# Two layers of hedgehog attention and mish: phi_q turned into tiles of its own, and five blocks of the first layer turned by VectorE

## The chip, the core and the metric

The kernel runs on one core of one Trainium2 chip. A core has TensorE (PE), which multiplies and writes to PSUM; VectorE (DVE), ScalarE (ACT) and GpSimd (POOL), which work elementwise; and SyncE (SP), whose queue issues all of this kernel's transfers. Every engine executes its own instructions in order and waits on semaphores for the others. The metric is device time of one execution in microseconds; of several runs the median counts.

## What is computed

Two identical layers follow each other on x (2048 tokens, 640 columns, fp32). Each is an attention step A and a dense step B, both with a residual and a layer norm ahead:

```python
x = x + _A_ref(_layernorm(x), A_wqkv, A_w_phi, A_wo)
x = x + _B_ref(_layernorm(x), B_w1, B_b1, B_w2)

def _A_ref(x, wqkv, w_phi, wo):              # 32 heads of 20 columns
    q, k, v = heads of x @ wqkv
    pq, pk = q @ w_phi, k @ w_phi            # per head
    phi_q = concat([softmax(pq), softmax(-pq)])
    phi_k = concat([softmax(pk), softmax(-pk)])
    kv, z = phi_k^T v, sum over tokens of phi_k
    return heads joined of (phi_q kv) / (phi_q z) @ wo

def _B_ref(x, w1, b1, w2):                   # 1536 hidden columns
    h = x @ w1 + b1
    return (h * tanh(softplus(h))) @ w2
```

## The kernel before

The 2048 tokens are worked in NB = 8 blocks of BLK = 256, and each block in BT = 2 tiles of 128 tokens (numbered i = 0 to 15). Weights and inputs are split into a high and a low part, and each product is made of three matmuls, so a projection of one token tile is 30 matmuls over 320 columns (`project`, L329; `project_half`, L338, whose matmul is L344).

A projection needs the normalized rows with the 640 columns on the partitions, that is, transposed. There are two ways to that:

- `normed` (L299) normalizes a block's rows on ACT into two row tiles `xn`, and `Transposed.step` (L271) transposes them on TensorE, 128 x 128 at a time (L280), ten transposes per block, into a PSUM tile `one`. ACT copies it to the high part `xth`, and VectorE subtracts to the low part `xtl` (L286).
- `spill_turned` (L311) transposes rows on VectorE within blocks of 32 x 32 (L315) and puts the blocks in their places by eight stores to DRAM in runs of 128 bytes (L317); `load_turned` (L319) reads them back in three loads (L325), and `Transposed.step` then takes `xth` and `xtl` from these SBUF tiles.

In the first layer's attention all eight blocks go the first way. In the second layer they go the second way: the end of the dense step before writes them (`n2_d`).

Each attention has two halves. `attend_first` (L381) goes over the blocks; in each, six steps project keys, values and queries of both token tiles (k0, k1, v0, v1, q0, q1; blocks 0 and 1 in other orders). What follows a projection is cut into stages by generators that are held in `pending`, and `advance` (L393) takes each one stage further after every step. `features` (L355) is shared by keys and queries: ACT copies the projection out of PSUM, VectorE takes maximum and minimum of every head (L368), two subtractions follow (L369 and L371), ACT exponentiates, VectorE sums (L377) and inverts (L378), and GpSimd multiplies (L379). For a key tile, 11 matmuls then add to the sums over tokens (L416). For a query tile, VectorE transposes the 128 x 1280 tile in place in 32 x 32 blocks (L425), and four stores of 160 KB each in runs of 128 bytes (L429) bring it to its block's tensor `e_d` in DRAM. Two query tiles (`r2_wide`, names `r210` and `r211`) take turns.

`attend_second` (L553) first finishes the sums (`finish_kv`, L532) and then, block by block, reads a block of `e_d` into two tiles of 1280 columns and a small one (`load`, L521), multiplies it with the sums and divides (`average`, L562, matmul L573), transposes the result on TensorE and projects it with wo. Loads of several blocks are under way ahead. The last queries (`rest`) are spread over its first steps.

What sets the order: ACT's work on the chain runs in program order (`act`, L110, chains each activation to the one before). All of the program stands in one block that the scheduler orders for each engine from its own model of the times. Inside `attend_second`, and in the opening of the first layer for SP, a hand-written order holds instead for TensorE and SP.

Buffers that take turns: `big` (1280 columns) has five, used for key tiles and for the loaded halves of `e_d`; `ol` (512 columns) has six; `x` (rows of a block) two; `xn` (640 columns) four; `mm`, the PSUM tile of a projection, two, and `one` four.

Of the kernel before, what the change touches and what calls it, by code (L numbers as in the profile page):

```python
# [42 lines left out]
def kernel(  # L43
# [266 lines left out]

    def spill_turned(rows, dst):  # L311

        dst = dst.rearrange("(j f) (t q s) -> t q f j s", f=32, t=BT, s=32)
        for t in range(BT):
            nc.vector.transpose(rows[t], rows[t])  # L315
            for q in range(4):
                nc.sync.dma_start(dst[t, q], rows[t][32 * q:32 * q + 32].rearrange("f (j s) -> f j s", s=32))  # L317

# [68 lines left out]
    def attend_first(layer, x_src, first):  # L387


        def fetch_normed(b):  # L390
            if layer:
                return load_turned(n2_d[b], [row_tile] * 3)
            xt = fetch(x_src, b)  # L393
            norm_scale(b, [norm_stats(t, xt) for t in range(BT)])
            return xt

        pending = []

        def advance():
# [21 lines left out]
        def queries(xts, i, ps=None):  # L421
            e = query_tile(i)
            yield from features(project(xts, i % BT, q_ws, 0) if ps is None else ps, e, True)

            nc.vector.transpose(e, e)  # L425
            b, t = divmod(i, BT)
            dst = e_d[b].rearrange("(j f) (t q s) -> t q f j s", f=32, t=BT, s=32)
            for q in range(4):
                nc.sync.dma_start(dst[t, q], e[32 * q:32 * q + 32].rearrange("f (j s) -> f j s", s=32))  # L429
                if b == NB - 1:  # L430
                    yield

        def values(xts, i, v):
# [30 lines left out]
        for b in range(NB):  # L464
# [9 lines left out]
            for n, (kind, t) in enumerate(order):  # L474
# [46 lines left out]
    def load(b):  # L521

        ta, tb, tc_ = big_tile(), big_tile(), pair_tile(F32)
        for t, g0 in ((ta, 0), (tb, 5)):

            src = e_d[b][120 * g0:120 * (g0 + 4) + P]
            src = bass.AP(tensor=src.tensor, offset=src.offset, ap=[[BLK, P], [120 * BLK, 5], [1, BLK]])
            nc.sync.dma_start(t.rearrange("f (g s) -> f g s", s=BLK), src)
        nc.sync.dma_start(tc_[:80, 0], e_d[b][1200:])
        return [(ta, tb)[g // 5][:, (g % 5) * BLK:(g % 5 + 1) * BLK] for g in range(10)] + [tc_[:, 0]]  # L530

    def finish_kv(kva, kvz, mask):  # L532

        acc, acz = row_tile(), row_tile()
        for src, dst, p1, n, w in ((kva, acc, P, 4, 120), (kvz, acz, P, 1, 120), (kvz, acz, 42, 1, 80)):
            c = 120 if w == 80 else 0
            nc.vector.tensor_tensor(dst[:p1, c:c + n * w].rearrange("p (n w) -> p n w", n=n),
                                    src[:p1, c:c + n * w].rearrange("p (n w) -> p n w", n=n),
                                    mask[:p1, :w].unsqueeze(1).to_broadcast([p1, n, w]), op=ALU.mult)
        yield  # L540
        for src, q0, n in ((acc, 0, 4), (acz, 4, 2)):
            ps = one_tile().rearrange("p (n c) -> p n c", n=4)
            for q in range(n):
                p1, w = (P, 120) if q0 + q < 5 else (42, 80)
                nc.tensor.transpose(ps[:w, q, :p1], src[:p1, 120 * q:120 * q + w], ident[:p1, :p1])  # L545
            if n == 4:
                act(kvb[:, :4], ps[:120], AF.Copy)
            else:
                nc.vector.tensor_copy(kvb[:, 4], ps[:120, 0])
                nc.vector.tensor_copy(kvb[:80, 5, :42], ps[:80, 1, :42])  # L550
        yield

    def attend_second(x_src, x_dst, acc, fetches, makes, fetch_next, begin_next):  # L553
# [9 lines left out]
        def average(b, t):  # L563
# [3 lines left out]
            for g in range(G):  # L567
                n = 120 if g < 10 else 80
                w = GW if g < 10 else 42
                c, j = divmod(g, 8)  # L570
                for q in range(2):
                    s0 = t * P + 64 * q
                    nc.tensor.matmul(  # L573
                        po[64 * q:64 * q + 64, c, GW * j:GW * j + w], phs[g][:n, s0:s0 + 64],
                        kvb[:n, g // 2, 64 * (g % 2):64 * (g % 2) + w], start=True, stop=True)
# [105 lines left out]
    def dense(x_src, x_dst, w1s, w2s, first, last):  # L681
# [58 lines left out]
        def end(b):  # L740
# [21 lines left out]
            if not last:  # L762
                xn = [row_tile() for _ in range(BT)]
                normalize(b, xn, [xt[:, t, :] for t in range(BT)])
                spill_turned(xn, n2_d[b])

# [132 lines left out]
```

## Time and profile before

| | us |
|---|---|
| runs, median of 3 | 1398.32 (1397.06 to 1398.65) |
| the profiled execution | 1396.09 |
| its span | 1394.3 |
| first layer: first half of attention | 0 to about 265 |
| first layer: second half of attention | about 265 to 375 |
| first layer: dense step | about 375 to 720 |
| second layer: first half of attention | about 720 to 942 |
| second layer: second half of attention | 942 to 1052 |
| second layer: dense step | 1052 to 1394 |

The profile shows one execution. Its rows give the start or the busy time in us, the engine, the line of the kernel, the operation, what it writes and reads (out<-in, by the names of the program), the shape, and the count; in brackets stands the idle time of the engine ahead of it and what ended it. "mean ns" follows the busy time where rows are grouped. The groups of the page that name the tiles of this change:

```profile
L280 PE MATMUL one<-ident,xn 128*128 128x128 f32 x260 | 37.2, 279 | 0.0
L429 SPq DMA_DIRECT2D e_d<-r x128: 302/885/3631, 59.6 to 1001.7; - x128
L317 SPq DMA_DIRECT2D n_d<-xn x176: 302/537/2272, 385.9 to 1317.1; - x176
```

The first is a group by form, with busy us and mean ns; matmuls are pipelined, so that the mean is longer than the pitch. The other two are the queue's own rows by line: shortest, median and longest time of one issue in ns, and the first and last start.

### The profile page before, as it was taken

The page shows a single profiled execution, that of the slowest core. Times are in us where ns is not written, and L with a number is a line of the kernel's source. Part 1 is how long each engine was busy: PE and PEld are TensorE (multiplying, and loading weights), DVE is VectorE, ACT ScalarE, POOL GpSimd, SP SyncE. Part 2 cuts the span into 40 slices and gives each one's busy share as a digit, 9 for nine tenths or more (in the row PEclk, how much of TensorE's full clock was granted, in tenths as well). Part 3 has the DMA queues.
Part 4 walks back from the last instruction along what each step waited for, and adds up shares of the span by engine and source line. Part 5 has one row for each costly group of instructions (what it writes and reads, how often), then busy time and mean ns, then how long its engine had stood idle before and what let it go on. Part 6 is the DMA issues. An engine that isn't in the chain of part 4 may idle for free. (4 is left out here: it accounts for less than half of the span.)

```text
span 1394.3 us, 28137 instructions
## 1 busy us (share of the span) xinstructions
PE 1380.7 (99%) x11528; PEld 1367.0 (98%) x11528; DVE 1075.5 (77%) x1820; ACT 583.3 (42%) x973; POOL 440.0 (32%) x334
## 2 busy tenths in 40 slices
PE   7999999999999999999999999999999999999998
PEld 7999999999999999999999999999999999999998
DVE  5797877796698877788769988888767876777775
ACT  4444433321355454545454333332235444444443
POOL 1353443343422221222234434343342211211112
PEclk9999999999999999999999999999999999999999
DMA  8533333689633432343474333357976212333200
GB/s 328 162 79 54 67 52 58 184 228 307 235 86 95 114 84 62 83 114 95 122 261 87 71 57 58 65 107 231 288 257 200 76 25 72 95 95 95 75 22 20
DMA packets 350035, 169.57 MB, mean 122 GB/s; under 512 B 286866, under 2 KB 323458, under 8 KB 349906
## 3 DMA queue, kind: packets, MB, share of 16 engines
q1 hardware_dynamic: 349906, 167.78, 44.2%
q8 instruction: 90, 1.47, 0.4%
q14 instruction: 39, 0.32, 0.1%
HBM read 104.82 MB, written 62.91 MB: 120 GB/s over the span
## 5 line engine op out<-in xcount | busy, mean ns | idle before, releaser
L737 PE MATMUL mm<-r2h,ol 128*128 128x320 f32 x1280 | 304.7, 309 | 0.0
L721 POOL TENSOR_TENSOR ol<-big,ol 128x512 fp32r<-128x512 f32 (+1 forms) x98 | 129.8, 1324 | 483.5 <-ACT ol L720 407.3
L695 PE MATMUL one<-xtl,r1h 128*128 128x256 f32 x960 | 268.2, 279 | 0.0
L695 PE MATMUL one<-xth,r1l 128*128 128x256 f32 x960 | 268.0, 279 | 0.0
L695 PE MATMUL one<-xth,r1h 128*128 128x256 f32 x960 | 265.9, 279 | 0.0
L737 PEld LDWEIGHTS mm<-r2h,ol 128*128 128x128 f32 x1280 | 219.1, 188 | 0.0
L737 PE MATMUL mm<-r2l,ol 128*128 128x320 f32 x640 | 197.3, 309 | 0.0
L344 PE MATMUL mm<-r1h,xth 128*128 128x320 f32 x600 | 187.3, 312 | 0.0
L344 PE MATMUL mm<-r1h,xtl 128*128 128x320 f32 x600 | 186.0, 310 | 0.7 <-DVE xtl L286 0.7
L344 PE MATMUL mm<-r1l,xth 128*128 128x320 f32 x600 | 186.0, 310 | 0.0
L695 PEld LDWEIGHTS one<-xtl,r1h 128*128 128x128 f32 x960 | 180.4, 188 | 0.0
L695 PEld LDWEIGHTS one<-xth,r1l 128*128 128x128 f32 x960 | 180.4, 188 | 0.0
L695 PEld LDWEIGHTS one<-xth,r1h 128*128 128x128 f32 x960 | 179.6, 188 | 0.0
L710 DVE TENSOR_SCALAR big<-big 128x512 f32<-128x512 f32 (+1 forms) x98 | 57.1, 583 | 109.9 <-ACT big L708 109.7
L379 POOL TENSOR_TENSOR r<-r,r 128x1280 f32<-128x1280 f32 x32 | 75.8, 2368 | 163.1 <-DVE r L378 157.3
L737 PEld LDWEIGHTS mm<-r2l,ol 128*128 128x128 f32 x640 | 120.2, 188 | 0.0
L712 ACT ACTIVATE big<-big,two 128x512 f32<-128x512 f32 (+1 forms) x98 | 70.1, 715 | 116.2 <-DVE big L711 116.1
L708 ACT ACTIVATE big<-one,b1s 128x256 f32<-128x256 f32 x192 | 80.8, 467 | 90.1 <-PE one L695 89.6
L720 ACT ACTIVATE ol<-big 128x512 fp32r<-128x512 f32 (+1 forms) x98 | 61.0, 622 | 136.0 <-DVE big L719 135.9
L344 PEld LDWEIGHTS mm<-r1h,xth 128*128 128x128 f32 x600 | 112.8, 188 | 1.3
L344 PEld LDWEIGHTS mm<-r1h,xtl 128*128 128x128 f32 x600 | 112.7, 188 | 1.3 <-DVE xtl L286 1.0
L344 PEld LDWEIGHTS mm<-r1l,xth 128*128 128x128 f32 x600 | 112.8, 188 | 0.1
(129 smaller groups left out, 3156.1 us busy)
## 6 DMA issues: line engine op xcount, KB each, us to landing
e_d<-r SPq DMA_DIRECT2D x128, 160.0 KB, 4.0
big<-e_d SPq DMA_DIRECT2D x32, 640.0 KB, 6.6
x_d<-xt SPq DMA_DIRECT2D x23, 640.0 KB, 3.9
xt<-x_d SPq DMA_DIRECT2D x22, 640.0 KB, 4.3
n_d<-xn SPq DMA_DIRECT2D x176, 80.0 KB, 2.1
xt<-in_x SPq DMA_DIRECT2D x16, 640.0 KB, 5.9
xn<-x_d SPq DMA_DIRECT2D x28, 320.0 KB, 4.2
v<-n_d SPq DMA_DIRECT2D x30, 256.0 KB, 3.3
```

What stands on the lines that cost most here:

```text
L344: nc.tensor.matmul(ps[:, :HC], a[:, sl], r, start=(k == 0 and n == 0), stop=(k == KD - 1 and n == 2))
L379: nc.gpsimd.tensor_tensor(eg, eg, r.unsqueeze(2).to_broadcast([P, 2 * H, DH]), op=ALU.mult)
L695: nc.tensor.matmul(ph[:, j, :], l, r, start=(n == 0), stop=(n == 3 * KD - 1))
L708: exps[0] = nc.scalar.activation(part(ta, 0)[:, j - js.start], ph[:, j, :], AF.Exp, bias=b1s[:, 2 * pr + j:2 * pr + j + 1]).ins
L710: nc.vector.tensor_scalar_min(e, e, E_CAP)
L712: nc.scalar.activation(r, n, AF.Ln, bias=two)
L720: nc.scalar.activation(ah[:, js], n, AF.Copy)
L721: nc.gpsimd.tensor_tensor(al[:, js], n, ah[:, js].bitcast(F32), op=ALU.subtract)
L737: nc.tensor.matmul(pys[t][:, c, :HC], l[:, j, sl], r, start=(f == 0 and n == 0), stop=(f == KF - 1 and n == 2))
```

## The change

In both layers:

- Query tiles of blocks 0 to 6 are no longer transposed in place. When the first tile of a block is ready, three tiles are taken (`blocks[b]`: two of the `big` buffers and 192 columns of an `ol` buffer), and VectorE transposes each query tile in three pieces into them, two of 640 columns (four blocks of 32 for each of five groups, the groups 120 columns apart, so that 8 columns are read twice) and one of 96, with strided sources and destinations (L476 of the changed kernel). After the block's second tile, twelve stores bring the three tiles to `e_d` and `f_d` in runs of 1280 and 256 bytes. Block 7 goes as before, to a tensor `g_d`.
- `load` reads blocks 0 to 6 as whole tiles, in runs of 5120 bytes; the last group has 96 rows instead of 80, the 16 others being met by zeros, for which `finish_kv` clears 16 columns.
- The tokens of a block stand in another order on the way, so `spill_turned` has a form for these tensors, and an input block that is transposed on TensorE is fetched in four transfers by 32 partitions.

In the first layer's attention alone:

- Blocks 0 to 2 are normalized and transposed on TensorE as before. Blocks 3 to 7 go through `turn`: rows are fetched, measured, normalized in place, transposed by VectorE and spilled to `n0_d` three blocks ahead of use, in stages that stand in the steps of the blocks between, and are then loaded as in the second layer.

```diff
+    def row_parts(t, b):
+        return t[b * BLK:(b + 1) * BLK, :].rearrange("(h t s u) d -> u h s t d", h=2, t=BT, u=2)
...
-    e_d = [dram.tile([EW, BLK], F32, name=f"e_d{b}") for b in range(NB)]
+    e_d = [dram.tile([2, P, EW], F32, name=f"e_d{b}") for b in range(NB - 1)]
+    f_d = [dram.tile([96, BLK], F32, name=f"f_d{b}") for b in range(NB - 1)]
+    g_d = dram.tile([EW, BLK], F32, name="g_d")
+    n0_d = [dram.tile([D, BLK], F32, name=f"n0_d{b}") for b in range(NB)]
...
     def attend_first(layer, x_src, first):
+        def fetch_parts(b):
+            xt = x_tile()
+            for q in range(4):
+                nc.sync.dma_start(xt[32 * q:32 * q + 32], row_parts(x_src, b)[q // 2, q % 2])
+            return xt
+
+        def turned(b):
+            return layer or b > 2
+
+        def turn(b):
+            xt = fetch(x_src, b)
+            yield
+            norm_scale(b, [norm_stats(t, xt) for t in range(BT)])
+            yield
+            rows = [xt[:, t, :] for t in range(BT)]
+            normalize(b, rows, rows)
+            yield
+            spill_turned(rows, n0_d[b], True)
+            yield
+
         def fetch_normed(b):
-            if layer:
-                return load_turned(n2_d[b], [row_tile] * 3)
-            xt = fetch(x_src, b)
+            if turned(b):
+                return load_turned((n2_d if layer else n0_d)[b], [row_tile] * 3)
+            xt = fetch_parts(b)
...
         def queries(xts, i, ps=None):
...
+            if t == 0:
+                blocks[b] = [big_tile(), big_tile(), pair_tile(F32).rearrange("p j s -> p (j s)")[:, :192]]
+            for c, dst in enumerate(blocks[b]):
+                src = e[:, EW - 96:].rearrange("p (j f) -> p j f", f=32)
+                if c < 2:
+                    src = e[:, 600 * c:600 * c + 600]
+                    src = bass.AP(tensor=src.tensor, offset=src.offset, ap=[src.ap[0], [32, 4], [120, 5], [1, 32]])
+                    dst = dst.rearrange("p (m g t s) -> p t m g s", m=4, t=BT, s=32)[:, t]
+                else:
+                    dst = dst.rearrange("p (j t s) -> p t j s", t=BT, s=32)[:, t]
+                nc.vector.transpose(dst, src)
+            if t == BT - 1:
+                for q in range(4):
+                    qs = slice(32 * q, 32 * q + 32)
+                    for c, (src, dst, m) in enumerate(zip(blocks[b], (e_d[b][0], e_d[b][1], f_d[b]), (4, 4, 3))):
+                        nc.sync.dma_start(dst.rearrange("(m f) (q x) -> q f m x", m=m, q=4)[q],
+                                          src[qs].rearrange("f (m x) -> f m x", m=m))
+                del blocks[b]
...
                     if n == 0:
                         xt = fetch_normed(b + 1)
                     elif n == 2:
-                        nxt = xt if layer else normed(b + 1, xt)
+                        nxt = xt if turned(b + 1) else normed(b + 1, xt)
                     elif n > 2:
                         nxt.step()
+                if not layer:
+                    if 0 < b < NB - 2 and n in (1, 2, 3):
+                        next(ahead)
+                    if n == 4 and b + 3 < NB:
+                        ahead = turn(b + 3)
+                        next(ahead)
...
     def load(b):
+        if b < NB - 1:
+            for c, t in enumerate((ta, tb)):
+                nc.sync.dma_start(t, e_d[b][c])
+            nc.sync.dma_start(tc_, f_d[b])
+            groups = [t.rearrange("f (q g s) -> f g q s", q=4, g=5) for t in (ta, tb)]
...
     def finish_kv(kva, kvz, mask):
         acc, acz = row_tile(), row_tile()
+        nc.vector.memset(acz[:42, 120:136], 0.0)
```

More of the change, by code (lines that the diff above doesn't have):

```diff
@@ L316, in spill_turned @@
             for q in range(4):
-                nc.sync.dma_start(dst[t, q], rows[t][32 * q:32 * q + 32].rearrange("f (j s) -> f j s", s=32))
+                nc.sync.dma_start(dst[q % 2, 2 * t + q // 2] if first_stage else dst[t, q],
+                                  rows[t][32 * q:32 * q + 32].rearrange("f (j s) -> f j s", s=32))
     def load_turned(src, tiles):
@@ L397, in attend_first @@
         pending = []
+        blocks = {}
         def advance():
@@ L423, in queries @@
             yield from features(project(xts, i % BT, q_ws, 0) if ps is None else ps, e, True)
-            nc.vector.transpose(e, e)
             b, t = divmod(i, BT)
[L427 to L430, printed above, removed]
-                    yield
+            if b == NB - 1:
+                nc.vector.transpose(e, e)
+                dst = g_d.rearrange("(j f) (q t s) -> t q f j s", f=32, t=BT, s=32)
+                for q in range(4):
+                    nc.sync.dma_start(dst[t, q], e[32 * q:32 * q + 32].rearrange("f (j s) -> f j s", s=32))
+                    yield
+                return
+            if t == 0:
[10 more added lines that the diff above has]
+            if t == BT - 1:
+                for q in range(4):
+                    qs = slice(32 * q, 32 * q + 32)
[3 more added lines that the diff above has]
+                del blocks[b]
         def values(xts, i, v):
@@ L543, in finish_kv @@
             for q in range(n):
-                p1, w = (P, 120) if q0 + q < 5 else (42, 80)
+                p1, w = (P, 120) if q0 + q < 5 else (42, 96)
                 nc.tensor.transpose(ps[:w, q, :p1], src[:p1, 120 * q:120 * q + w], ident[:p1, :p1])
@@ L549, in finish_kv @@
                 nc.vector.tensor_copy(kvb[:, 4], ps[:120, 0])
-                nc.vector.tensor_copy(kvb[:80, 5, :42], ps[:80, 1, :42])
+                nc.vector.tensor_copy(kvb[:96, 5, :42], ps[:96, 1, :42])
         yield
@@ L567, in average @@
             for g in range(G):
-                n = 120 if g < 10 else 80
+                n = 120 if g < 10 else 96
                 w = GW if g < 10 else 42
```

27 lines of the change are left out of this document (14 added, 13 removed).

## Prediction

> **What bounds the kernel now.** I read the page's head and its chain first, then busy time by stage.
>
> ```profile
> span 1394.3 us, 28137 instructions
> PE 1380.7 (99%) x11528; PEld 1367.0 (98%) x11528; DVE 1075.5 (77%) x1820; ACT 583.3 (42%) x973; POOL 440.0 (32%) x334
> PE 44%; DVE 0%; issue 0%; DVEq 0%
> ```
>
> ```profile
> 0.00:12.00 12.00, 4.88 (x20) 4.37 (x20) 2.88 (x10) 2.18 (x3) 1.75 (x9) 1.00 0.84 282
> 12.00:58.00 46.00, 46.00 (x310) 44.20 (x310) 30.35 (x66) 24.22 (x48) 12.45 (x16) 1.00 0.74 276
> 58.00:114.00 56.00, 56.00 (x437) 54.75 (x436) 55.14 (x70) 25.45 (x35) 30.00 (x21) 1.00 0.41 79
> 114.00:225.00 111.00, 111.00 (x869) 109.69 (x869) 85.07 (x115) 43.73 (x63) 45.95 (x28) 1.00 0.29 49
> 225.00:330.00 105.00, 104.57 (x1189) 102.14 (x1188) 81.63 (x170) 29.14 (x44) 40.18 (x26) 1.00 0.77 206
> 773.00:948.00 175.00, 174.80 (x1358) 172.44 (x1358) 145.44 (x164) 61.99 (x88) 73.86 (x36) 1.00 0.42 77
> 948.00:1053.00 105.00, 104.57 (x1283) 102.44 (x1282) 77.25 (x209) 27.81 (x46) 42.41 (x39) 1.00 0.83 268
> ```
>
> The columns are the stretch, its length, and busy time of PE, weight loads, DVE, ACT and POOL, then the PE clock, the DMA share and GB/s. TensorE is the bound, at the full clock: of its 13.6 us idle, 7.1 lie in the first 12 us, and in the two stages where DMA is busiest (225 to 330, 948 to 1053) only 0.43 each. So nothing is gained by cheaper transfers; time is gained by taking matmuls away, and lost wherever TensorE is made to wait. The stretch to watch is 58 to 114 (blocks 1 and 2 of layer 0): VectorE is busy 55.14 of 56.00, and this change puts work there.
>
> **Term 1, the transposes taken from TensorE.** Five blocks of layer 0 lose ten 128x128 transposes each. Ten stand alone in the chain in order of time:
>
> ```profile
> 985.69 1.09 PE one L280 x10
> ```
>
> 50 x 0.109 = 5.45 us saved, on the path. That the group price carries over to transposes mixed among projections is the choice here; the bounds are 5 and 6.
>
> **Term 2, the start.** Block 0's input comes in four issues instead of one, ahead of the second half of the weights that the fold waits for:
>
> ```profile
> 2.58 0.43 SPq L384 DMA_DIRECT2D xt<-in_x  x1
> ```
>
> ```profile
> 10.37 2.04 PE L237 MATMUL mm<-big,raw 120*128 120x120 f32 x8 [2.46 <-DMA raw<-in_wqk_t]
> ```
>
> Three more issues at 0.43 are 1.3 us at most; the engines move data at 0.84 of their time there (row above), so part is hidden behind bytes that are still flowing. +0.5, from 0 to 1.3.
>
> **Term 3, VectorE between blocks 1 and 2 of layer 0.** The instruction order of the changed kernel, as built, shows what now stands before the second subtraction (L371) of key tile k1 of block 1. These are the rows of before around it:
>
> ```profile
> 85.07 0.76 DVE L371 TENSOR_TENSOR big<-m,big 128x640 f32<-128x640 f32 x1
> ```
>
> ```profile
> 85.92 1.27 ACT L116 ACTIVATE big<-big 128x1280 f32<-128x1280 f32 x1 [1.82 <-DVE big L371]
> 87.10 0.37 ACT L116 ACTIVATE xth<-one 128x256 fp32r<-128x256 f32 x1
> 87.36 0.26 ACT L116 ACTIVATE v<-ident 128x32 f32<-128x32 f32 x1
> 87.49 0.71 ACT L116 ACTIVATE v<-mm 128x640 f32<-128x640 f32 x1
> ```
>
> ```profile
> 88.99 1.38 PE L416 MATMUL one<-big,v 128*64 128x120 f32 x22
> ```
>
> and the prices:
>
> ```profile
> L315 DVE STREAM_TRANSPOSE xn<-xn 128x640 f32<-128x640 f32 x44 | 36.3, 834 | 2.0 <-ACT xn L116 1.9
> L425 DVE STREAM_TRANSPOSE r<-r 128x1280 f32<-128x1280 f32 x32 | 47.7, 1490 | 3.6 <-POOL r L379 3.4
> L250 DVE BATCH_NORM_STATS2 bn<-xt 128x6 f32<-128x320 f32 x60 | 25.1, 470 | 1.7 <-DMA xt<-in_x 1.7
> L377 DVE TENSOR_REDUCE r<-r 128x64 f32<-128x1280 f32 x32 | 47.1, 1473 | 0.0
> L368 DVE TENSOR_REDUCE m<-r 128x32 f32<-128x640 f32 x64 | 48.8, 803 | 26.7 <-ACT r L116 26.7
> L286 DVE TENSOR_TENSOR xtl<-one,xth 128x512 fp32r<-128x512 f32 x52 | 34.4, 672 | 2.9 <-ACT xth L116 2.5
> L286 DVE TENSOR_TENSOR xtl<-xn,xth 128x512 fp32r<-128x512 f32 x14 | 16.6, 1188 | 0.0
> ```
>
> Ahead of that subtraction there are now: the two transposes of block 3's turned rows (2 x 0.834 = 1.67); one more set of statistics, block 5's, because turning works three blocks ahead (4 x 0.470 = 1.88); one sum over 1280 columns (1.47) and one max/min pair (2 x 0.803 = 1.61) that the scheduler has moved forward; and two query tiles turned in three pieces. No row shows a transpose with strided operands. By columns, 1376 at 0.834 per 640 make 1.79 for a tile against 1.49, +0.30 each, 0.60 for two; the bounds are no dearer than now (0) and twice the price per column (+2.1 a tile). I take the column price, since the 640- and 1280-column rows nearly agree per column. The sum is 7.23, and VectorE has no idle here to hide it, so the subtraction ends at 85.83 + 7.2 = 93.0. ACT runs its chain in program order: the exponential that needs the subtraction, then xth, the ones, and the copy of v1's projection, 1.27 + 0.37 + 0.26 + 0.71 = 2.6, so that copy ends at 95.6. It frees the PSUM tile that the first half of block 2's k1 is written to, and in the order built TensorE reaches that projection right behind the key sums: 88.99 + 1.38 and some 0.4 = 90.8. Stall 4.8. On the way GpSimd's product for those same key sums also comes some 4 us late, which lies within the same wait. The bounds are 2 (moved work costs less than its mean) and 8 (block 5's rows, fetched only behind the spill of block 3, arrive after VectorE wants them). In the queue, a turned block adds one fetch, eight spills and three loads; the first load waits until all eight have landed, and behind it stand that fetch and the stores of an earlier block's phi. Only the fetch is wanted soon, by the statistics just counted; the turned rows themselves are loaded nearly a block (29 us) ahead of their projection, which hides them.
>
> Past that point VectorE has room again: blocks 3 to 7 use 85.07 of 111.00, 22.2 per 29.0 us block, and turning adds 1.67 + 0.60 + 2 x (1.188 - 0.672) = 3.3, which makes 25.5. I cost that at nothing, the cover being the 3.5 left; with strided transposes at double price another 3.6 would use it up.
>
> On the dearer xtl: the rows show 1188 ns where it reads xn and 672 where it reads PSUM. [...]
>
> **Term 4, the first loads of the second half, in both layers.** In the built order, the queue now holds twelve stores of block 6 behind one another, and two big tiles of that block are alive when block 0 is loaded. Five big buffers do not hold these, two key tiles and both halves of block 0, so block 0's second half waits for the key sums of the last block's k0. Before, it was block 1's second half that waited there:
>
> ```profile
> 266.91 0.38 SPq L528 DMA_DIRECT2D big<-e_d  x1
> ```
>
> ```profile
> 265.46 2.54 PE L416 MATMUL one<-big,v 128*64 128x120 f32 x44
> ...
> 271.25 1.38 PE L573 MATMUL mm<-kvb,big 120*64 120x63 f32 x40
> ...
> 274.45 1.38 PE L573 MATMUL mm<-kvb,big 120*64 120x63 f32 x40 [0.43 <-PE mm L573]
> ```
>
> ```profile
> e_d<-r SPq DMA_DIRECT2D x128, 160.0 KB, 4.0
> big<-e_d SPq DMA_DIRECT2D x32, 640.0 KB, 6.6
> ...
> xt<-x_d SPq DMA_DIRECT2D x22, 640.0 KB, 4.3
> n_d<-xn SPq DMA_DIRECT2D x176, 80.0 KB, 2.1
> ```
>
> Issued at 266.9, block 0's half lands at 271.2 (4.3, long runs) to 273.5 (6.6, runs of 1 KB); TensorE wants it half way through its first averages, at 271.9. Behind it stand four last stores of block 6, issued at 0.38 each until 268.8 and landed 2.1 to 4.0 later; block 1's loads reuse the buffers that these read, are issued at 270.5 to 272.7 and land at 275 to 279, wanted at 274.45 to 275.6. The stalls overlap: 2.2 per layer, from 0 to 4, 4.4 for two.
>
> **Term 5, layer 1.** Its blocks 0 to 2 already wait for GpSimd and VectorE:
>
> ```profile
> 768.84 1.38 PE L416 MATMUL one<-big,v 128*64 128x120 f32 x22 [0.35 <-POOL big L379]
> 772.10 1.04 DVE L286 TENSOR_TENSOR xtl<-xn,xth 128x256 fp32r<-128x256 f32 x1
> ```
>
> Two query tiles at +0.30 stand before that xtl: +0.5, from 0 to 2.
>
> At nothing: the longer last group (96 rows for 80, same columns), the cleared 16 columns, kvb's copy, the new token order of the spills (same issues and bytes). Of the stores, 8 issues per block of 128-byte runs become 12 of 1280: the queue's work shrinks, but no TensorE wait rests on it.
>
> **Sum.** -5.45 + 0.5 + 4.8 + 4.4 + 0.5 = +4.75 on the profiled execution's 1396.09, so 1400.8. That execution is 2.2 below the median of the runs, 1398.32; carried over to the median: 1403.0. Case A, chance 0.50, own range 1399 to 1407.
>
> **Rivals.** B, 0.18: nothing stalls; terms 3 to 5 find slack that I don't see, as VectorE's backlog did before (114 us in, it idles again). Then -5.45 + 0.5, with the transfers' idle of 2 x 0.43 gone at best: 1393. Against it: the rows that end term 3 leave TensorE's margin at 90.8 - 88.2, 2.6 us, for 7.2 of new work. [...]
>
> C, 0.21: only one of terms 3 and 4 decides, and transposes and stall cancel: -5.45 + 4.8 + 0.5 = -0.2, about 1398. For it: both hang on a few us of landing time or moved work.
>
> D, 0.11: strided transposes cost twice a column. From the point where VectorE's 25.5 passes the 29.0 that TensorE leaves it (+3.6), it bounds blocks 1 to 5 of layer 0: term 3 grows by two tiles, 3.6, and each of four blocks by some 0.5, layer 1 by 2: 1403 + 7.6 = 1410.6.
>
> **Numbers.** A change under 0.2%, 2.8 us, can't be told from none. A is slower in 0.42 of its 0.50, else the same; C the same in 0.15, slower and faster in 0.03 each; B faster; D slower. Faster 0.21, same 0.23, slower 0.56. The range 1394 to 1411 leaves out most of B's lower half and the end of D.
>
> **What would show it.** Term 1: the group of transposes at 210 for 260. Term 3: idle of TensorE of 3 to 7 us near 90 us, waiting for GpSimd at the key sums or for ACT at the projection behind them; VectorE without a gap from 55 to past 114. Term 4: TensorE waiting for a load from e_d some 6 us behind the last key sums, twice. D: strided transposes over 1.2 us per 640 columns. I am wrong if these waits are under 1 us each, or if a new wait stands where none is named.

## The result and the profile after

The changed kernel takes 1418.82 us, the median of 4 runs (1417.19 to 1424.65), against 1398.2 for the kernel before: ratio 1.0156, 95% interval 1.0126 to 1.0186. It is slower by 20.6 us where 4.7 were forecast, and it lies outside the forecast range of 1394 to 1411. The profiled execution took 1417.83 us, 21.74 above the profiled execution of before.

The page of the changed kernel:

```profile
span 1415.7 us, 28191 instructions
...
PE 1385.2 (98%) x11478; PEld 1368.4 (97%) x11478; DVE 1097.1 (77%) x1888; ACT 584.3 (41%) x973; POOL 447.4 (32%) x334
...
PE 83%; DVE 9%; DMA 3%; issue 2%; POOL 2%; ACT 1%; SPq 0%; DVEq 0%; POOLq 0%; ACTq 0%
```

TensorE has 50 matmuls fewer, as it should, and yet is busy 4.5 us longer; its idle time has grown from 13.6 to 30.5 us. Two things therefore cost time: waits, and matmuls that run slower. The stretches and the waits of TensorE show where (columns as in the prediction; the waits have their sum in us, how often, and the longest):

```profile
0.00:12.00 12.00, 3.60 (x12) 2.79 (x12) 1.18 (x5) 2.18 (x3) 0.68 (x6) 1.00 0.84 215
12.00:58.00 46.00, 43.72 (x280) 41.53 (x281) 27.15 (x66) 22.98 (x45) 10.32 (x16) 1.00 0.82 286
58.00:114.00 56.00, 53.10 (x402) 51.42 (x401) 54.91 (x79) 23.68 (x33) 28.72 (x20) 0.97 0.33 86
114.00:225.00 111.00, 105.38 (x780) 103.32 (x779) 97.86 (x131) 42.76 (x61) 48.02 (x28) 0.98 0.46 106
225.00:330.00 105.00, 102.24 (x1115) 99.56 (x1114) 88.64 (x163) 32.49 (x46) 42.34 (x26) 0.98 0.54 162
```

```profile
PE one L449 <- POOL big L389: 8.0, 3, 2.9
PE mm L246 <- DMA raw<-in_wqk_t: 6.9, 4, 4.4
PE mm L354 <- DVE xtl L295: 6.0, 4, 4.2
PE mm L246 <- DVE bn L259: 3.5, 1, 3.5
```

Three stretches that had the full clock before now show 0.97 and 0.98. Narrower stretches, laid on the places, resolve it:

```profile
97.70:101.10 3.40, 3.40 (x26) 2.90 (x23) 3.40 (x9) 2.27 (x4) 2.38 (x1) 0.50 0.34 80
...
193.20:196.60 3.40, 3.03 (x11) 3.03 (x12) 2.91 (x5) 0.00 (x0) 2.58 (x2) 0.51 0.91 203
282.00:285.40 3.40, 3.40 (x27) 3.19 (x26) 1.51 (x4) 1.27 (x1) 0.00 (x0) 0.50 0.84 268
964.70:968.10 3.40, 3.40 (x15) 3.32 (x14) 0.79 (x3) 0.65 (x1) 0.00 (x0) 0.51 0.70 225
```

The third column from the end is TensorE's granted clock. Behind four waits it is halved for 3.4 us, which adds up to 1.7 us to each: up to 6.8 of the 21.4 us by which the span grew.

Laying the two traces on each other gives the whole account. The projections' matmuls stand in the same order in both but for swaps of near ones (L354 here, L344 before), so the start of the n-th one here less its start before is TensorE's delay up to that point:

| place (us of before) | delay there | change | of it, fewer transposes | loss |
|---|---|---|---|---|
| start, to 57 | 5.31 | +5.31 | 0 | 5.3 |
| blocks 1 and 2, to 118 | 8.89 | +3.58 | -1.09 | 4.7 |
| blocks 3 and 4, to 178 | 7.79 | -1.10 | -2.18 | 1.1 |
| block 5, to 208 | 13.76 | +5.97 | -1.09 | 7.1 |
| to 254 | 12.65 | -1.11 | -1.09 | 0 |
| end of the first half, first layer | 16.67 | +4.02 | 0 | 4.0 |
| dense step and second layer, to 940 | 16.87 | +0.20 | 0 | 0.2 |
| end of the first half, second layer | 21.40 | +4.53 | 0 | 4.5 |

Losses of 26.9 less 5.45 are 21.4, the growth of the span. The second half of each attention and both dense steps lose nothing.

At the start, the first projection begins at 21.9 us instead of 17.3. TensorE's waits ahead of it make 3.2 of these 4.6 us (10.4 instead of 7.1). The rest is work at half rate: until 22.6 us the matmuls of L246 follow each other every 213 ns, behind that every 112 ns; in the kernel before, this step comes at 16.6 us. The 1.00 that the first rows show for the clock doesn't hold there, as the trace has no record of the clock before that step.

### The profile page after: what moved, and what is told of

It reads as the page before. It is cut to its first block, busy times and chain, and to the rows that moved or that the text cites. A ratio compares the mean times of both kernels' runs of the same rounds, so it can differ in the third digit from the quotient of the medians.

```text
span 1415.7 us, 28191 instructions
## 1 busy us (share of the span) xinstructions
PE 1385.2 (98%) x11478; PEld 1368.4 (97%) x11478; DVE 1097.1 (77%) x1888; ACT 584.3 (41%) x973; POOL 447.4 (32%) x334
## 4 chain that ended last, share of the span: by engine, by line
PE 83%; DVE 9%; DMA 3%; issue 2%; POOL 2%; ACT 1%; SPq 0%; DVEq 0%; POOLq 0%; ACTq 0%
PE mm L802 24%; PE one L760 24%; PE mm L354 16%; PE one L354 12%; PE mm L638 3%; PE one L449 2%; DVE r L387 2%; PE one L289 2%; DVE m L378 1%; DVE big L379 1%; POOL big L389 1%; DMA raw<-in_wo 1%; DVE big L476 1%; DMA raw<-in_wqk_t 1%; DMA xt<-in_x 1%
## 5 line engine op out<-in xcount | busy, mean ns | idle before, releaser
L354 PE MATMUL mm<-r1h,xtl 128*128 128x320 f32 x600 | 186.6, 312 | 6.0 <-DVE xtl L295 6.0
L354 PE MATMUL mm<-r1h,xth 128*128 128x320 f32 x600 | 187.8, 313 | 0.8 <-ACT xth L125 0.3
L354 PE MATMUL mm<-r1l,xth 128*128 128x320 f32 x600 | 186.5, 311 | 0.0
L389 POOL TENSOR_TENSOR r<-r,r 128x1280 f32<-128x1280 f32 x32 | 79.5, 2484 | 168.8 <-DVE r L388 148.8
L354 PEld LDWEIGHTS mm<-r1h,xtl 128*128 128x128 f32 x600 | 113.2, 189 | 7.7 <-DVE xtl L295 7.0
L354 PEld LDWEIGHTS mm<-r1h,xth 128*128 128x128 f32 x600 | 113.5, 189 | 2.8 <-ACT xth L125 0.8
L354 PEld LDWEIGHTS mm<-r1l,xth 128*128 128x128 f32 x600 | 113.6, 189 | 0.4
```

The source lines that it names most:

```text
L354: nc.tensor.matmul(ps[:, :HC], a[:, sl], r, start=(k == 0 and n == 0), stop=(k == KD - 1 and n == 2))
L389: nc.gpsimd.tensor_tensor(eg, eg, r.unsqueeze(2).to_broadcast([P, 2 * H, DH]), op=ALU.mult)
```

## How VectorE falls behind near 190 us

The largest loss stands where the prediction named none. The last two waits for `xtl` there, 0.81 and 4.21 us, are TensorE's:

```profile
187.21 0.41 PE L354 MATMUL mm<-r1h,xtl 128*128 128x320 f32 x1 [0.81 <-DVE xtl L295]
...
193.57 0.64 PE L354 MATMUL mm<-r1h,xtl 128*128 128x320 f32 x1 [4.21 <-DVE xtl L295]
```

VectorE in order of time, and SP's queue over the same block:

```profile
160.74 0.54 DVE L388 RECIPROCAL r<-r 128x64 f32<-128x64 f32 x1
165.02 1.67 DVE L259 BATCH_NORM_STATS2 bn<-xt 128x6 f32<-128x320 f32 x4 [3.74 <-DMA xt<-in_x]
...
192.54 0.98 DVE L295 TENSOR_TENSOR xtl<-xn,xth 128x256 fp32r<-128x256 f32 x1
```

```profile
148.87 5.15 SPq L326 DMA_DIRECT2D n_d<-xt  x8
156.38 1.40 SPq L335 DMA_DIRECT2D xn<-n_d  x3
157.83 0.43 SPq L394 DMA_DIRECT2D xt<-in_x  x1
```

The fetch at 157.83 stands behind a spill and behind the load that waits until the spill has landed. The scheduler has put the statistics of these rows (L259) where it expects them to have landed; VectorE, in order, waits there 3.74 us, and 3.47 a block earlier. The work on these rows isn't wanted by TensorE for two more blocks, but the `xtl` behind them is wanted at once. From one third `xtl` to the next VectorE takes 32.7 us (160.82 to 193.52), TensorE 29.06 for a block.

VectorE also has more to do than was counted. By form, 114 to 225 us, changed kernel and then before (busy us, mean ns):

```profile
L476 DVE STREAM_TRANSPOSE big<-r 128x640 f32<-128x640 f32 x14 | 10.9, 816 | 0.8 <-POOL r L389 0.8
L295 DVE TENSOR_TENSOR xtl<-xn,xth 128x512 fp32r<-128x512 f32 x8 | 10.7, 1336 | 0.1
...
L379 DVE TENSOR_TENSOR big<-big,m 128x640 f32<-128x640 f32 x7 | 8.4, 1207 | 0.0
...
L295 DVE TENSOR_TENSOR xtl<-xn,xth 128x256 fp32r<-128x256 f32 x4 | 4.4, 1112 | 0.0
```

```profile
L369 DVE TENSOR_TENSOR big<-big,m 128x640 f32<-128x640 f32 x8 | 6.4, 799 | 0.0
...
L286 DVE TENSOR_TENSOR xtl<-one,xth 128x512 fp32r<-128x512 f32 x6 | 4.1, 677 | 0.0
```

The strided transposes cost what their columns say (816 ns per 640). But `xtl` costs 1336 ns where 1188 was taken, its third piece 1112 ns, which was left out, and the subtraction of the keys went from 799 to 1207 ns. Of the groups in this stretch, all that grew by over 1% read two SBUF operands; reductions (797 and 800 ns for 640 columns against 815 and 814, 1474 and 1450 for 1280 against 1478 and 1438) and transposes of 640 columns (816 against 834 for L315 before) did not. The means hide two kinds: of the eight `xtl` of 512 columns four took 0.62 to 0.68 us and four 1.78 to 2.40, and beside each of the latter a GpSimd product or subtraction ran for 1.2 us or more, beside the former for 0.4 at most. Not every instruction with two SBUF operands suffers: the second subtraction of the keys (L381) took 786 ns, and 817 before.

## Experiments

Theory T: five separate causes, at the start, near 97 us, near 190 us and at the two ends, each with the loss of the table. Rivals stand with each run. Times are medians beside runs of the kernel before on the same chip; "loss" is taken from the delay between the traces, as above.

**phi_q alone.** `turned(b)` returns `layer`, and the calls of `turn` go.

> The phi_q part alone; all eight blocks of the first layer are normalized and transposed on TensorE again. Theory T (the 20.6 us are separate stalls: 5.3 at the start, from the input fetched by 32 partitions; some 5.4 near 97 us and 8 between 155 and 209 us, both from turning; 4.0 and 4.5 behind the last key sums of the two layers, from phi_q's own VectorE order): no stall near 97 and 190, the start and both ends stay, so 1398.3 + 5.3 + 4.0 + 4.5 + 0.2 = about 1412. Rival (phi_q's transposes alone saturate VectorE and cause the stalls inside the first layer too): 1419 or more, since the 5.45 of transposes taken from TensorE are given back.

Measured: 1412.77, ratio 1.0105 (1.009 to 1.012). As T has it, from 118 to 254 us the delay stands still at 12.70, and the ends lose 3.7 each. Near 97 us 1.4 remain of the 4.7, which T did not expect. The start lost 11.3 in the profiled execution, the slowest of four (1415.84): the first projection begins at 22.65 us, hardly later than in the changed kernel, but its matmuls still take 0.47 us instead of 0.31, and the full rate comes only at 35.7 us.

**Turning alone**, built into the kernel before.

> The kernel before plus the turning of blocks 3 to 7 alone; queries as before, input in single transfers. Theory T: the start and the two ends are as before, transposes save 5.45, the stalls near 97 us and near 190 us come at most in full: 1398.3 - 5.45 + 5.4 + 8 = 1406, and less (down to 1396) as far as the queue is not held up by twelve stores per block. Rival (the stalls need both parts, VectorE has room for turning alone): 1393 to 1394.

Measured: 1411.46, ratio 1.0093 (1.0076 to 1.011); neither expectation holds. Its waits:

```profile
PE mm L345 <- ACT r L117: 7.0, 4, 2.1
...
PE mm L345 <- DVE xtl L287: 3.4, 4, 1.3
```

Without phi_q's tiles ScalarE waits for a query tile whose stores stand behind eight stores of a spill in the queue (44.9 us in six waits between 50 and 220 us), and TensorE for ScalarE. So the two halves of the change aren't independent: phi_q's tiles take away a wait that turning brings.

**The fetch earlier.** `ahead = turn(b + 3)` from the fifth step to the first, from block 2 on.

> The changed kernel, but from block 2 on the input that is to be turned is fetched in the first step of a block instead of the fifth, so that in the queue it stands before the spill and the load that waits for the spill. Theory T (VectorE, in order, waits 3.5 us per block for that fetch, and this uses up its room): VectorE's waits for the input vanish after 130 us, and the 8 us between 155 and 209 with them: about 1411. Rival (VectorE simply has too much work in blocks 3 to 5): the stall near 190 stays, 1417 to 1419.

Measured: 1418.78, ratio 1.0145 (1.013 to 1.016). The edit did not do what it was to do: the fetch is still issued at 158.72, behind the load, because its `x` tile (two in turn) is free only when the spill has landed. It tells nothing about T.

**The input in one transfer.**

```diff
-            for q in range(4):
-                nc.sync.dma_start(xt[32 * q:32 * q + 32], row_parts(x_src, b)[q // 2, q % 2])
+            return fetch(x_src, b, xt)
...
-                        nc.tensor.transpose(ps[:, c, t * P:(t + 1) * P],
+                        dst = ps[:, c].rearrange("p (t u h s) -> p u h t s", t=BT, u=2, s=32)[:, t]
+                        nc.tensor.transpose(dst,
```

> The changed kernel, but blocks 0 to 2 are fetched in one transfer over all 128 partitions each, and the token order is made by where TensorE's transposes write in PSUM. Theory T (transfers into 32 partitions slow everything that moves beside them: 240 instead of 370 GB/s in the first 20 us): the first projection is back at 17.3 to 17.8 us instead of 21.9, about 1414. Rival (the new order itself, or VectorE's statistics, delay the start): 1418 to 1419.

Measured: 1414.94, ratio 1.0118 (1.0103 to 1.0133). T holds: the first projection starts at 18.1, and at 57 us the delay is 1.6 instead of 5.3. But the loss near 97 us grew from 4.7 to 7.7: the projection behind that stall (the 450th matmul) starts at 112.8 us instead of 113.5, although the start came 3.7 us sooner. VectorE reaches the key subtraction there 2.5 us sooner, not 3.7, so the late start had covered part of the stall: TensorE's waits grow from 2.9 to 4.1 us, and the clock is at half for 6.8 us behind them instead of 3.4.

**Two runs on why the start is slow**: the input by 64 partitions, and, on top of the run before, by alternate rows over all partitions.

```diff
-            for q in range(4):
-                nc.sync.dma_start(xt[32 * q:32 * q + 32], row_parts(x_src, b)[q // 2, q % 2])
+            parts = x_src[b * BLK:(b + 1) * BLK, :].rearrange("(h t s u) d -> t u h s d", h=2, t=BT, u=2)
+            for u in range(2):
+                for t in range(BT):
+                    nc.sync.dma_start(xt[64 * u:64 * u + 64, t, :], parts[t, u])
```

> The changed kernel, but the input of blocks 0 to 2 comes in four transfers over 64 partitions each instead of four over 32: the same count of issues, the same bytes, the same runs of 2560 bytes. Theory T (a transfer into few partitions slows all that move beside it): the first projection starts between 17.8 and 20 us instead of 21.9, and packets of 2560 bytes take 120 to 150 ns instead of 173 between 8 and 16 us. Rival (the count of issues): 21.5 to 22, packets as slow as now.

> The kernel with the input of blocks 0 to 2 in single transfers and the order made by TensorE's writes, but each of these transfers cut in two: every second row to one half of the columns, so packets of 2560 bytes from alternate rows, as in the changed kernel, yet over all 128 partitions. Theory T (few partitions make transfers slow): the first projection starts at 18.1 to 18.7 us and packets of 2560 bytes take about 105 ns between 8 and 16 us. Rival (alternate rows or shorter runs are slow): 20.5 to 22 us and 150 ns or more.

One execution each: 1448.48 and 1417.33 us. The stretch from 8 to 16 us (for the 64 partitions also 16 to 24), in the order before, changed, 64 partitions, alternate rows; the last two columns are the DMA share and GB/s:

```profile
8.00:16.00 8.00, 5.63 (x25) 5.38 (x26) 5.70 (x19) 4.17 (x8) 1.31 (x5) 1.00 1.04 372
```

```profile
8.00:16.00 8.00, 3.75 (x15) 2.94 (x14) 3.12 (x10) 1.66 (x3) 1.09 (x3) 1.00 1.01 222
```

```profile
8.00:16.00 8.00, 0.56 (x3) 0.27 (x2) 0.53 (x1) 0.90 (x2) 0.00 (x0) 1.00 0.51 146
16.00:24.00 8.00, 1.70 (x7) 1.70 (x8) 2.68 (x9) 0.43 (x1) 1.09 (x3) 1.00 0.13 49
```

```profile
8.00:16.00 8.00, 5.71 (x25) 5.13 (x25) 5.60 (x19) 3.83 (x7) 1.28 (x4) 1.00 1.04 357
```

In the changed kernel the engines are as busy as before (1.01) and move 222 GB/s instead of 372: a packet of 2560 bytes takes 173 ns instead of 104 (medians of that stretch). Packets of 480 and 1440 bytes, which are not the input's, took 39 and 116 ns instead of 26 and 89, so what moves beside the input is slowed too. Alternate rows over all partitions are back at 357 GB/s and 105 ns, as theory T has it, though the first projection starts at 19.7 us, between the two expectations. So neither the rows nor the length of runs is the cause. What is left is the few partitions; that these transfers are also four for a block instead of two or one was not tested by itself. The run with 64 partitions refutes both of its expectations: the first projection starts at 43.1 us. Its transfers also have an outermost dimension of 2, and from 16 to 24 us the trace shows a share of 0.13, as much as two engines of sixteen, at 49 GB/s. Whether that dimension is the cause was not tested, so the run can't tell what 64 partitions do as such.

**The statistics held back.** Placed behind the second key tile's maximum (`tc.issue_after`), in step 2; normalizing and spilling in steps 3 and 4.

> The changed kernel, but the statistics of a block that is to be turned stand on VectorE behind the second key tile's maximum, some 10 us later than now, when their rows have long landed; normalizing and spilling follow one step later each. Theory T (the in-order wait of 3.5 us per block for the late fetch uses up VectorE's room): the waits of VectorE for the input (3.5 and 3.7 us at 131 and 161 us) vanish, the 8.2 us that TensorE loses between 155 and 209 us vanish with them: about 1411. Rival (turning is too much work for VectorE, wherever it stands): the loss near 190 us stays, 1416 to 1419.

Measured: 1425.28, ratio 1.0189 (1.0172 to 1.0206). VectorE's waits for the input are gone, as meant, but the wait has changed engines:

```profile
ACT xt L125 <- DVE stats L271: 24.9, 4, 6.4
```

Normalizing stands in ScalarE's program order ahead of the copies that TensorE needs, and waits there for the statistics. So the run couldn't decide; the next one moves normalizing too.

**The statistics held back, normalizing two steps later** (`next(now)` in steps 4 and 5).

```diff
-                    if 0 < b < NB - 2 and n in (1, 2, 3):
-                        next(ahead)
+                    if 0 < b < NB - 2 and n in (4, 5):
+                        next(now)
...
                 advance()
+                if not layer and 0 < b < NB - 2 and n == 2:
+                    now = ahead
+                    with tc.issue_after(reduced[0]):
+                        next(now)
```

> The changed kernel with the statistics of a block to be turned behind the second key tile's maximum, as in the earlier run, and normalizing (on ScalarE, in program order) and spilling two steps behind that, so that neither VectorE waits for the input nor ScalarE for the statistics. Theory T (the waits of 3.5 and 3.7 us for the input are what VectorE cannot afford): the stall near 190 us is under 2 us, 1410 to 1412. Rival (VectorE is full with the work alone): a loss of 4 us or more between 155 and 209 us, 1415 to 1419.

Measured: 1414.16, ratio 1.0116 (1.0086 to 1.0147), with a wide spread of runs (1411.7 to 1420.3). The stretch of blocks 3 to 6:

```profile
114.00:225.00 111.00, 108.82 (x824) 106.58 (x824) 106.73 (x148) 45.63 (x65) 54.91 (x35) 1.00 0.48 104
```

The loss from 148 to 208 us of before is 1.1 instead of 8.2 (3.0 if the next 7 us, where another 1.9 go, are counted in), in small pieces, and the clock is full. So T holds for the stall, but its time was missed: the profiled execution lost 6.4 at the start and 5.2 and 5.3 at the ends. The row also gives VectorE's busy time where it holds TensorE up little: 106.73 of 111.00, 27.9 for each 29.06 us block.

**Less work for VectorE** (`lean` from block 3 of the first layer on).

```diff
-        for s, op in ((0, ALU.max), (1, ALU.min)):
+        for s, op in ((0, ALU.max), (1, ALU.min))[:1 if lean else 2]:
...
-        nc.vector.tensor_tensor(eh[:, 1], m[:, 1].unsqueeze(2)
+        nc.vector.tensor_tensor(eh[:, 1], m[:, 0 if lean else 1].unsqueeze(2)
```

> The changed kernel with work taken from VectorE alone: in blocks 3 to 7 of the first layer the minimum of every head is left out (the maximum serves for both), four reductions of 0.74 us a block, 2.9 of the 28 to 29 us that VectorE is busy per block there. Nothing else moves. Theory T (VectorE's own work plus its waits exceeds TensorE's 29.06 us per block between 125 and 195 us): the stall near 190 us and its half clock vanish, 7 to 8 us of the loss between 155 and 209: about 1411. Rival (the wait for the late fetch, 3.5 us in each block, sets it whatever VectorE has to do): a loss of 4 us or more stays there, 1415 or more.

Measured: 1416.01, ratio 1.0124 (1.0101 to 1.0147). From 148 to 208 us it loses 4.9 where the changed kernel loses 8.2. By its numbers the rival holds, with 4 us or more left and 1415 or more; the half clock near 190 us is gone, as T had it. So both count: 2.9 us less work per block take away 3.3 of the loss; the waits for the input are still there (7.6 us in 3), and the rest of the loss with them. (This execution's start lost 10.4, with the clock at half for 10.2 us from 23 us on.)

**The tail of VectorE's order.** The transposes of block 6's second query tile are put behind the reciprocal of the last key tile.

```diff
+            if b == NB - 2 and t == BT - 1:
+                yield
...
-                nc.vector.transpose(dst, src)
+                    with tc.issue_after(inverted[0]):
+                        nc.vector.transpose(dst, src)
```

> The changed kernel, but in both layers the transposes of the second query tile of block 6 stand on VectorE behind the reciprocal of the last key tile instead of ahead of its sum. Theory T (at the two ends TensorE waits for GpSimd's product, late because VectorE waits 2.1 us for the other product ahead of those transposes): the product of the last key tile comes 5 us sooner, the waits of 2.3 and 2.8 us and the clock's 1.7 each vanish: 1418.8 - 8 = 1411. Rival (the load of block 0's second half, term 4 of the prediction, then takes the place of that wait, 2.2 per layer): 1414 to 1416.

Why it was tried stands in the changed kernel's rows at the end of the second layer's first half:

```profile
952.79 0.95 DVE L388 RECIPROCAL r<-r 128x64 f32<-128x64 f32 x2
953.47 2.37 POOL L389 TENSOR_TENSOR r<-r,r 128x1280 f32<-128x1280 f32 x1 [7.71 <-DVE r L388]
...
955.87 1.57 DVE L476 STREAM_TRANSPOSE big<-r 128x640 f32<-128x640 f32 x2 [2.14 <-POOL r L389]
...
957.53 1.44 DVE L387 TENSOR_REDUCE r<-big 128x64 f32<-128x1280 f32 x1
...
960.34 0.54 DVE L388 RECIPROCAL r<-r 128x64 f32<-128x64 f32 x1
960.71 0.34 SPq L584 DMA_DIRECT2D big<-e_d  x1
961.01 2.36 POOL L389 TENSOR_TENSOR big<-big,r 128x1280 f32<-128x1280 f32 x1
...
963.42 1.39 PE L449 MATMUL one<-big,v 128*64 128x120 f32 x22 [2.77 <-POOL big L389]
```

VectorE waits 2.14 us for GpSimd's product of the query tile, turns it, and only then sums the last key tile, for which TensorE waits. Measured: 1425.52, ratio 1.0198 (1.0182 to 1.0213), slower than the changed kernel. The wait for GpSimd is gone from both ends, and this stands in its place:

```profile
PE mm L646 <- DMA big<-e_d: 10.0, 4, 4.3
```

In the first layer the last store of block 6 is issued at 285.3 us instead of 282.1, but the first load of block 1 is issued at 285.88, hardly later than in the changed kernel (285.58). TensorE, without the wait for the product, is ready for it at 287.6 instead of 290.8, and waits 4.35 us. Behind these waits the clock is at half for 6.8 us in the first layer and 10.2 in the second; the ends lose 6.7 and 8.1. Neither expectation foresaw that it would get worse, though the rival named the wait.

**Block 6 the old way too**: `if b >= NB - 2` in place of `b == NB - 1`, and a `g_d` for each.

> The changed kernel, but block 6 too goes the old way: transposed in place and stored in runs of 128 bytes, so that the tail of both first halves is as in the kernel before, without the two tiles of block 6 and their twelve stores. Theory T (both ends, 4.0 and 4.5 us, are due to block 6's transposes and tiles standing there): the ends lose less than 1 us each, 1418.8 - 8 = about 1411. Rival (VectorE reaches the end late for another reason, or the loads are late anyway): 1416 to 1419.

Measured: 1413.83, ratio 1.0108 (1.0084 to 1.0131). The ends lose 0 and 0.6: T holds for the ends, and both the product's wait and that of the loads are gone. The median lies above T's 1411, with runs from 1409.86 to 1417.03.

**Turning from block 4 on.**

> The changed kernel, but block 3 goes over TensorE as blocks 0 to 2 do, and turning begins with block 4. Theory T (the stall near 97 us is block 3's transposes and block 5's statistics on a saturated VectorE): it vanishes, ten more transposes cost 1.09, 1418.8 - 5.4 + 1.1 = 1414.5. Rival (the stall moves one block on, to 125 us, or comes from phi_q's transposes): 1418 to 1420.

Measured: 1417.19, ratio 1.0132 (1.0117 to 1.0147). In the trace the loss between 57 and 118 us is 2.6 instead of 4.7, without a halved clock, and does not move one block on; the stall near 190 us stays (7.1). So T holds in part, and the gain in time is within the spread of the runs.

**Do the causes add up?** The single transfers, the held statistics and block 6 the old way together; the same with turning from block 4; and each half of the change by itself, mended.

> The changed kernel with three edits of the earlier runs together: input of blocks 0 to 2 in single transfers, statistics and normalizing held back, block 6 the old way. Theory T (the causes are separate and add up): start 0.8, near 97 us 3 to 7, nothing near 190, no loss at the ends, transposes -5.45, some 1 to 2 of small waits: 1398.5 + 0 to 5.5, about 1399 to 1404. Rival (what is won at one place is lost at the next, as VectorE is too full in any case): 1407 or more.

> The same three edits, and turning from block 4 on. Theory T: the crowding of VectorE between blocks 1 and 2 is gone too (2.6 instead of 3 to 7 at most), transposes -4.36: 1398.5 + 0.8 + 0 to 2.6 + 1 to 2 - 4.36, about 1396 to 1400. Rival: the stall moves one block on, 1403 or more.

> The kernel before with turning alone, statistics and normalizing held back as in the earlier run. In the run of turning alone TensorE lost 3.6 us near 70 us and 10 between 160 and 211, waiting for ScalarE, which waited for query tiles whose stores stood in the queue behind the eight stores of a spill. Theory T: the hold takes away only VectorE's wait, the stores behind the spill stay: 1404 to 1411. Rival (the late fetch was the cause there too): 1393 to 1398.

> phi_q alone (no turning), input of all eight blocks of the first layer in single transfers, block 6 the old way. Theory T (of phi_q's cost only the start and the two ends count): start 0.8, 1.4 near 100 us, ends 0, the second layer 0.2: 1398.5 + 2.4 = about 1401. Rival (strided transposes cost more in the blocks between): 1404 or more.

| | median us | ratio, interval |
|---|---|---|
| three edits | 1398.11 | 1.0001, 0.9992 to 1.001 |
| three edits, turning from 4 | 1396.54 | 0.9987, 0.9978 to 0.9996 |
| turning alone, held | 1402.73 | 1.0032, 1.0021 to 1.0043 |
| phi_q alone, mended | 1399.92 | 1.0009, 1.0 to 1.0018 |

The three edits together take 20.7 us from the changed kernel, and its clock stays full. That is more than their medians gained one by one (3.9, 4.7 and 5.0), and the time lies a little under T's 1399 to 1404. One by one, each edit left the other stalls and halved clocks standing, and some of these grew. So the causes are separate places in the trace, but the single gains in time don't measure them. With turning from block 4, as T has it, the median (11 runs against 29) is 1.7 us under that of the kernel before, 0.13%, and the interval just leaves out 1: the one version here that beats it. Its profiled execution, span 1394.4, isn't ahead of the 1394.3 of before, which was a quick one. Its waits are down to

```profile
PE mm L246 <- DMA raw<-in_wqk_t: 7.8, 3, 4.6
PE mm L356 <- ACT r L125: 1.5, 1, 1.5
PE mm L356 <- ACT xth L125: 0.9, 1, 0.9
```

Against the 4.36 us of its 40 fewer transposes stand 1.2 at the start, 1.4 near 104 us and 2.0 in small waits up to 254 us. phi_q alone costs about 1.6 even when mended, near T's 2.4, so it brings nothing by itself. Its use is beside turning: 1398.11 with it against 1402.73 for turning alone, held. That fits the freed query tiles: in turning alone, held, ScalarE still waits 28.9 us for their stores between 50 and 220 us, and TensorE 3.5 us for ScalarE and 4.5 for `xtl`. That run fell between its two expectations; how much of its loss is the stores behind the spill was not separated.

## Why the prediction was wrong

- Term 1, right: 210 transposes for 260, and 1.09 us less per block in the delays.
- Term 2, mis-sized: 0.5 (0 to 1.3) was forecast, 5.3 came. The price was taken from the issue (0.43 each), and the bytes were held to flow as fast as before. The step "three more issues at 0.43 are 1.3 us at most" fails: the cost lay in the transfers, which move at 222 GB/s instead of 372, and in the half rate, at which TensorE works until 22.6 us instead of 16.6.
- Term 3, right in place and mechanism, in size by luck: 4.8 forecast, 4.7 measured. VectorE was late, and with it GpSimd's product and ScalarE's copy, which ends at 100.4 us where 95.6 and the later start make 100.9. But TensorE's wait ended with the product, which the forecast had inside the wait for the copy, and was 2.90; the halved clock, which the forecast did not have, made up the rest.
- "I cost that at nothing, the cover being the 3.5 left" is the step that failed most: 8.2 us from 118 to 208. VectorE needs 27.9 of 29.06 us, not 25.5, and the waits of 3.5 to 3.7 for the fetch, which the prediction bounded only for block 5's rows near 90 us, go beyond the 1.1 that are left. Holding the statistics back, with no work taken away, brought the 8.2 down to 1.1 (3.0 by 215 us). And from 114 to 225 us an `xtl` of 512 columns took 1336 ns, where 1188 was taken and the kernel before has 677: four of eight were long (1.78 to 2.40 us), each beside 1.2 us or more of GpSimd's work, and four took 0.62 to 0.68.
- Term 4, right in place, mis-sized, and the wait that ended last was another: 4.4 for both layers (2.2 each, a choice between 0 and 4), 8.5 measured, of which 3.4 are the clock. TensorE waited for GpSimd's product, behind VectorE's new order. That the forecast wait for the loads was there too, hidden, is shown by the run that took the other away: its loads are issued at nearly the same time, and TensorE waits 10.0 us for them in four waits, for block 1's and not, as forecast first, for block 0's.
- Term 5: 0.5 forecast, 0.2 measured.
- Rival D had a VectorE without room, but for a wrong reason: strided transposes cost 0.82 us per 640 columns, not twice a column. At 1410.6 it was still 8 us short.

In sum, of the 16.7 us by which the forecast missed the trace, 8.2 are the loss that none of the terms had, 4.8 the start and 4.1 the ends; terms 3 and 5 were 0.4 too dear.

## What to carry to other kernels

Where an engine is counted at 88% of the bound's period (25.5 of 29.0), the rest isn't all cover: every wait that the change puts into its order, and every instruction that gets dearer by its new operands (`xtl` here, from 677 to 1336 ns), is taken from it first. An in-order engine should not do work for two blocks ahead in front of work for now, unless its data have surely landed (VectorE waited 3.47 and 3.74 us here); hold such work back, and everything behind it on the other engines as well. And price a split transfer by where it lands (32 partitions here, in a stretch with 222 GB/s instead of 372), not by its issues.

## What the runs showed of the hardware

- Behind four stalls of TensorE of 2.3 to 4.2 us in one piece in the changed kernel, the clock was at half for 3.4 us, which costs up to 1.7 us more each; in other runs it was at half for 6.8 and 10.2. Here 2.04 (phi_q alone), 2.33, 2.77 and 2.90 us of idle in one piece were enough, while 2.32 and 2.77 in the run with normalizing later were not: that execution's mean clock is 1.00. So the length of the stall alone does not tell whether the clock drops.
- The kernel begins at half rate: matmuls of L246 every 213 ns instead of 112, until 16.6 us in the kernel before, 22.6 in the changed one and 35.7 in the profiled execution of phi_q alone. So the late start of the changed kernel cost 3.2 us of waits and some 1.3 of half rate up to its first projection.
- With the input in transfers into 32 partitions, the engines moved 222 GB/s from 8 to 16 us, against 357 to 372 with transfers over 128, weights being in the mix each time. What moved beside the input was slower too (480-byte packets of other transfers took 39 ns instead of 26).
- In the run by 64 partitions, whose input transfers have an outermost dimension of 2, the DMA share was 0.13 from 16 to 24 us, at 49 GB/s, and the first projection started 25.7 us late, at 43.1 us; which property of the transfers did it was not tested.
